# Efficient attention followed by a two-layer MLP: batch 0's k less its maxima on VectorE, its small transfers queued behind large ones, two x tiles of batch 1 turned by DMA, and a new order

## Chip, cores, metric

One Trainium2 chip, one of its cores. The metric is the device time of one execution in microseconds (us); where several runs of a kernel are given, their median. Engines are named as the profile names them: PE (TensorE), DVE (VectorE), ACT (ScalarE), POOL (GpSimd) and SP (SyncE, which here only issues transfers).

## What is computed

Eight batches, eight heads, 576 rows, head size 64; inputs and output are float32.

```python
def _attn_ref(q, k, v):
    q_s = np.exp(q - np.max(q, axis=-1, keepdims=True))
    q_s = q_s / (np.sum(q_s, axis=-1, keepdims=True) + 1e-09)
    k_s = np.exp(k - np.max(k, axis=2, keepdims=True))          # maxima over the rows
    k_s = k_s / (np.sum(k_s, axis=2, keepdims=True) + 1e-09)
    kv = np.einsum('bhsd,bhse->bhde', k_s, v)
    return np.einsum('bhsd,bhde->bhse', q_s, kv)

def _moe_ref(x, g_ln, w_ch1, w_ch2):                            # x: (8, 576, 512)
    mu = np.mean(x, axis=-1, keepdims=True)
    var = np.mean((x - mu) ** 2, axis=-1, keepdims=True)
    xn = (x - mu) / np.sqrt(var + 1e-06) * g_ln
    return x + np.maximum(xn @ w_ch1, 0.0) @ w_ch2              # 512 -> 2048 -> 512
```

## The kernel before

**Tiling.** Of a batch's 576 rows, 512 are held as four tiles of 128 (j = 0 to 3); the last 64 rows of two batches make a fifth tile (j = 4) together. The MLP runs in nine chunks: one for each batch's 512 rows, and a ninth for the left-over rows.

**An order written out by hand.** All the work is a table of tasks `T[(name, batch, part)]`, built in `batch(m)`, `chunk(ci)` and `weights()`. The string `PROGRAM` names every task once; `write_all` goes through it and issues each task's instructions on its engine. Each engine works through its own instructions strictly in that order, and a transfer stands in the queue of the engine that issues it; the engine can be given as in `kll.1@SP`. Waits between engines follow from the data. A word is name.batch.part:

- `kl`, `ql`, `vl`: loads of the 512 rows of k, q, v (1 MB for a batch, in rows of 1 KB; batch 0's are cut by heads into parts of 512 or 256 KB). `kll`, `qll`, `vll`: the 64 left-over rows (128 KB in 512 pieces of 256 bytes). `g`: the norm's weights (0 load, 1 turn, 2 copy). `w1l`, `w2l`: the weights of the two layers, four parts of each, issued by POOL and cast to bf16 on the way.
- `kmax`, `kmaxl` (DVE): maxima of k over the tiles, and with the left-over rows. `kar` (POOL): the same over the partitions. `ksub`, `kexp` (DVE, ACT): subtraction and exponential. `vc`: v cast to bf16.
- `qmax`, `qsub` (DVE), `qexp` (ACT): the same for q. `qT` (PE) and `qTe` (copy) turn q's exponentials; `qTd` does it by DMA on SP. `zpe` sums them on PE (line 361), `zq` on DVE (lines 353 and 354); where `zpe` is used, `zq` is only a reciprocal (line 366).
- `pkv` (PE), `kvb` (DVE): k times v, scaled. `po` (PE), `x` (DVE): the attention's output, scaled, with its row sum. `xn`: x less its mean. `xT` (PE, line 474) with `xTe`/`xTf` (copies) turn it; by DMA it is one transfer on SP (line 500). `sq`, `rstd` (ACT): the norm's factor.
- `l1`, `relu`, `l2`, `put`, `store`: the two layers, the result and its store. `w1s`: layer 1's weights times the norm's weights, for the later chunks. For batches 0 and 1, layer 1 comes in parts l1.batch.c.t: l1.1.8.0 and those after it need all four tiles.
- `warm`: matmuls with no result that is used. `gate.i` (SP): a transfer of a few bytes which waits for a given task (gate.0 for qexp.0.0), so that what stands behind it on SP's queue is issued only then.

**Batch 0's k.** For a pair of heads c below `KPE`, `kid` (line 222) brings k to PSUM through an identity matmul on PE, the task `ksub` is `kless` (line 230), which subtracts the maxima there by a second matmul, and `kexp` reads PSUM. For the other pairs `ksub_pair` (line 235) subtracts on DVE, in place. KPE is 3 of 4 pairs. `KPARTS` cuts k's loads and maxima into heads 0-3, 4-5 and 6-7.

**Sums and turned tiles.** `ZPE = 2`: batches 0 and 1 use `zpe`. `by_dma` says which tiles a DMA turns: from batch 2 on, and the fifth tile.

Of the kernel before, what the change touches and what calls it, by code (L numbers as in the profile page):

```python
# [20 lines left out]
def kernel(  # L21
# [594 lines left out]
    def warm(n, width):  # L616
# [26 lines left out]
        l1.0.1.2 qsub.1.0 l1.0.0.2 qmax.1.2 relu.0.1.2 relu.0.1.3 l1.0.1.0 relu.0.0.2 w1s.0@DV
        l1.0.1.1 relu.0.1.0 qsub.1.2 l1.0.11.0 relu.0.1.1 l1.0.9.0 relu.0.11.0 kmax.1.0 l1.0.8.0
        l1.0.10.0 relu.0.8.0 relu.0.9.0 l1.0.14.0 l1.0.15.0 relu.0.14.0 relu.0.10.0 l1.0.13.0
        kmaxl.1.0 qexp.1.0 w1s.2@DV l1.0.12.0 kar.1.0 relu.0.15.0 l2.0.0 relu.0.13.0 relu.0.12.0
        l2.0.1 w2l.2 ksub.1.0 qexp.1.2 l2.0.2 ksub.1.1 qT.1.0 vc.1.2@PO l2.0.3 qTe.1.0@DV kexp.1.1
        w2l.3 l2.0.4 ksub.1.2 kexp.1.0 qT.1.2 zpe.1.0 l2.0.5 qTe.1.2@DV kexp.1.2 w1s.1@DV
        vc.1.0@AC vc.1.1@PO l2.0.6 ql.2.0@AC zpe.1.2 l2.0.7 sq.0.3 w1s.3@DV pkv.1.0 sq.0.0 pkv.1.1
        sq.0.2 l2.0.8 kvb.1.0 sq.0.1 l2.0.9 zq.1.0 zq.1.2 kl.2.0@AC po.1.2 rstd.0 po.1.0 po.1.3  # L650
        x.1.2 po.1.1 l2.0.10 x.1.0 x.1.1 l2.0.11 xn.1.0@AC gate.4 x.1.3 xn.1.1@AC l2.0.12 kll.2@SP
        xn.1.2@AC kl.3.0@SP l2.0.13 vl.2.0@SP qmax.2.0 xT.1.0 l2.0.14 xTe.1.0@AC put.0.0 l2.0.15
        put.0.1 xn.1.3@AC put.0.2 l1.1.0.0 sq.1.1 qsub.2.0 xT.1.2 relu.1.0.0 l1.1.1.0 xTe.1.2@AC
        put.0.3 l1.1.2.0 kmax.2.0 relu.1.1.0 qexp.2.0 l1.1.3.0 l1.1.8.0 ql.3.0@AC qTd.2.1
        kmaxl.2.0 relu.1.2.0 l1.1.9.0 qmax.2.2 relu.1.3.0 kar.2.0 vll.2@SP l1.1.10.0 relu.1.9.0
        qTd.2.0 qsub.2.2 relu.1.8.0 l1.1.11.0 relu.1.10.0 qll.1.1@SP ksub.2.2 l1.1.12.0
        relu.1.11.0 ksub.2.0 qexp.2.2 l1.1.13.0 relu.1.12.0 ksub.2.1 l1.1.14.0 qTd.2.2 relu.1.13.0
        l1.1.15.0 relu.1.14.0 zq.2.0 qTd.2.3 l1.1.0.2 relu.1.15.0 zq.2.2 l1.1.1.2 vc.2.1
        relu.1.0.2 kexp.2.0 kll.3@SP l1.1.2.2 vc.2.0 kexp.2.1 l1.1.3.2 qll.1.0@SP qmax.3.0 l2.1.0
        kexp.2.2 kll.4@SP vc.2.2 sq.1.3 store.0.0@SP kmax.3.0 l2.1.1 vl.3.0@SP relu.1.2.2 pkv.2.0  # L660
        store.0.2@SP relu.1.1.2 pkv.2.1 sq.1.0 l2.1.2 kvb.2.0 sq.1.2 l2.1.3 store.0.1@AC po.2.3
        store.0.3@AC po.2.1 qmax.1.4 po.2.0 po.2.2 x.2.3 l2.1.4 x.2.0 xn.2.3@AC l2.1.5 kmaxl.3.0
        xn.2.0@AC xT.2.3 l2.1.6 x.2.2 relu.1.3.2 kar.3.0 x.2.1 l2.1.7 xn.2.2@AC xT.2.0 qsub.3.0
        xn.2.1@AC l2.1.8 rstd.1 xT.2.2 ksub.3.0 l2.1.9 qexp.3.0 l2.1.10 put.1.0 xT.2.1 l2.1.11
        ksub.3.1 vll.3@SP l2.1.12 vc.3.0 put.1.1 kexp.3.1 kl.4.0@SP l2.1.13 qsub.1.4 l2.1.14
        put.1.2 qexp.1.4 l2.1.15 kexp.3.0 store.1.2@SP qTd.1.4 l1.2.0 put.1.3 vc.3.2 l1.2.1
        qmax.3.2 relu.2.0 vc.3.1 ql.4.0@SP l1.2.2 qTd.3.0 relu.2.1 ksub.3.2 l1.2.3 relu.2.2
        qsub.3.2 store.1.0@SP l1.2.4 qTd.3.1 relu.2.3 zq.1.4 kexp.3.2 l1.2.5 qexp.3.2 zq.3.0
        l1.2.6 relu.2.4 qTd.3.3 l1.2.7 relu.2.6 zq.3.2 relu.2.5 pkv.3.0 gate.2 relu.2.7 po.1.4
        pkv.3.1 kll.5@SP sq.2.3 x.1.4 l1.2.8 kmax.4.0 l1.2.9 relu.2.8 qTd.3.2 l1.2.10 qmax.4.0  # L670
        l1.2.11 relu.2.10 ql.5.0@SP relu.2.9 l1.2.12 kmaxl.4.0 gate.3 relu.2.11 kvb.3.0 l1.2.13
        kar.4.0 relu.2.12 vl.4.0@SP sq.2.0 store.1.3@SP l1.2.14 qmax.4.2 relu.2.13 l1.2.15
        xn.1.4@AC l2.2.0 sq.2.1 relu.2.15 po.3.1 po.3.0 relu.2.14 po.3.3 po.3.2 l2.2.1 x.3.3 x.3.2
        l2.2.2 xn.3.3@DV xn.3.2@AC x.3.1 l2.2.3 sq.2.2 qsub.4.0 xT.3.2 l2.2.4 rstd.2 x.3.0 sq.3.2
        l2.2.5 xT.3.3 ksub.4.0 xn.3.0@AC l2.2.6 store.1.1@AC xT.3.0 put.2.0 l2.2.7 sq.3.3 ksub.4.1
        xn.3.1@AC l2.2.8 kexp.4.0 xT.3.1 vc.4.1 l2.2.9 ksub.4.2 qexp.4.0 l2.2.10 vll.4@SP vc.4.0
        qmax.5.0 kexp.4.1 kl.5.0@SP l2.2.11 gate.0 put.2.1 kexp.4.2 l2.2.12 qTd.4.0 qsub.4.2
        l2.2.13 l2.2.14 put.2.2 qexp.4.2 vc.4.2 qmax.5.2 l2.2.15 qTd.4.3 l1.3.0 put.2.3 qTd.4.2
        l1.3.1 zq.4.0 pkv.4.0 relu.3.1 store.2.1@SP pkv.4.1 relu.3.0 l1.3.2 qTd.4.1 kvb.4.0 l1.3.3
        relu.3.2 kmax.5.0 kl.6.0@SP l1.3.4 qll.3.1@SP relu.3.3 kll.6@SP qll.3.0@AC l1.3.5 sq.3.1  # L680
        zq.4.2 l1.3.6 relu.3.4 relu.3.5 l1.3.7 kmaxl.5.0 store.2.0@AC qsub.5.2 l1.3.8 relu.3.6
        kar.5.0 l1.3.9 relu.3.8 qsub.5.0 po.4.2 po.4.1 relu.3.9 l1.3.10 relu.3.7 sq.3.0 po.4.0
        po.4.3 l1.3.11 x.4.0 rstd.3 ksub.5.1 relu.3.10 l1.3.12 vl.6.0@AC l1.3.13 x.4.1 relu.3.11
        relu.3.12 xn.4.0@DV l1.3.14 ksub.5.2 relu.3.13 xT.4.0 x.4.3 l1.3.15 relu.3.14 ksub.5.0
        vl.5.0@SP sq.4.1 l2.3.0 store.2.2@SP relu.3.15 x.4.2 l2.3.1 xn.4.1@AC xn.4.3@DV kmax.6.0
        l2.3.2 qexp.5.0 xT.4.3 l2.3.3 xT.4.1 l2.3.4 kmaxl.6.0 xn.4.2@DV l2.3.5 kar.6.0 qmax.3.4
        xT.4.2 l2.3.6 qsub.3.4 put.3.0 l2.3.7 gate.1 qexp.3.4 qTd.5.1 kexp.5.0 ksub.6.2 l2.3.8
        ksub.6.1 qexp.5.2 l2.3.9 store.2.3@SP kexp.5.1 l2.3.10 vll.5@SP vc.5.0 vll.6@SP l2.3.11
        kexp.6.1 vc.6.0 qTd.3.4 l2.3.12 kexp.6.2 put.3.2 vc.5.1 kexp.5.2 l2.3.13 zq.3.4 ql.6.0@SP
        put.3.1 l2.3.14 vc.6.1 kl.7.0@SP ksub.6.0 l2.3.15 qTd.5.2 vc.5.2 l1.4.0 qTd.5.3 put.3.3  # L690
        kexp.6.0 l1.4.1 vc.6.2 zq.5.0 relu.4.0 l1.4.2 qTd.5.0 relu.4.1 l1.4.3 zq.5.2 store.3.2@SP
        l1.4.4 relu.4.3 store.3.1@SP relu.4.2 pkv.5.0 relu.4.4 pkv.6.0 pkv.5.1 kll.7@SP pkv.6.1
        po.3.4 l1.4.5 x.3.4 l1.4.6 kvb.5.0 qll.5.1@SP l1.4.7 qmax.6.0 relu.4.6 relu.4.5 po.5.1
        l1.4.8 qmax.6.2 relu.4.7 l1.4.9 store.3.3@SP relu.4.8 qsub.6.2 ql.7.0@SP l1.4.10 relu.4.9
        x.5.1 l1.4.11 relu.4.10 qsub.6.0 sq.1.4 l1.4.12 relu.4.11 l1.4.13 kvb.6.0 l1.4.14 kmax.7.0
        relu.4.13 relu.4.12 l1.4.15 qexp.6.2 po.5.0 po.5.2 l2.4.0 qexp.6.0 x.5.2 qTd.6.2 l2.4.1
        x.5.0 relu.4.14 relu.4.15 xT.1.4 xn.5.0@DV l2.4.2 kmaxl.7.0 sq.4.0 po.5.3 xn.5.1@AC
        kar.7.0 l2.4.3 x.5.3 qTd.6.3 sq.4.2 l2.4.4 xn.5.3@DV sq.4.3 zq.6.0 l2.4.5 xT.5.3
        store.3.0@AC rstd.4 l2.4.6 xn.5.2@AC zq.6.2 xT.5.0 l2.4.7 sq.5.3 sq.5.0 l2.4.8 xT.5.2
        ksub.7.1 l2.4.9 ksub.7.0 xT.5.1 kexp.7.1 l2.4.10 put.4.0 l2.4.11 kexp.7.0 qll.5.0@SP  # L700
        vll.7@SP l2.4.12 store.4.0@AC qTd.6.1 put.4.2 sq.5.1 l2.4.13 put.4.1 qll.7.1@SP l2.4.14
        qTd.6.0 l2.4.15 vl.7.0@SP l1.5.0 put.4.3 vc.7.2 l1.5.1 ksub.7.2 relu.5.0 l1.5.2 relu.5.1
# [474 lines left out]
```

## Time and profile before

| | |
|---|---|
| median of 3 runs | 293.98 us (293.83 to 294.09) |
| the profiled execution | 294.13 us, its span 292.3 us |
| granted clock of PE, mean | 0.993 |
| PE, DVE, ACT, POOL busy | 282.2, 182.9, 170.7, 50.1 us |
| first product of layer 1 (line 550) | 23.31 us from the span's start |
| first product of layer 2 (line 590) | 38.12 us |
| end of PE's work | 288.74 us |
| read from memory, written | 36.70 MB, 9.44 MB |

The span is from the first to the last instruction. A view of waits names for each instruction what the idle time of its engine ended with; the chain follows the last instruction back through such releasers. A transfer's time to landing counts from its issue. Queue q1 is SP's, q10 ACT's, q0 POOL's. In lines of the timeline the columns are start, duration, engine, line, operation, out<-in, shape and count, and in brackets the idle time before.

### The profile page before, as it was taken

The numbers are of one execution on the slowest core, as the hardware profiler recorded it, in microseconds if no ns is written. First come the engines' busy times: TensorE is split into PE (matmuls) and PEld (weight loads), VectorE is DVE, ScalarE is ACT, GpSimd is POOL, SyncE is SP. The second block draws the span as 40 slices with busy tenths as digits, with TensorE's granted clock in tenths as the row PEclk, the third lists the DMA queues.
The fourth block names the chain that finished last, engine by engine and source line by source line (L and its number), as shares of the span: only waits on it lengthen the run. The fifth ranks groups of instructions, "written<-read, shape, count | busy, mean of one in ns | idle before, by whom it ended". The sixth has DMA issues, their size and how long they took to land.

```text
span 292.3 us, 4988 instructions
## 1 busy us (share of the span) xinstructions
PE 282.2 (97%) x1934; PEld 146.9 (50%) x1964; DVE 182.9 (63%) x309; ACT 170.7 (58%) x319; POOL 50.1 (17%) x51
## 2 busy tenths in 40 slices
...
GB/s 191 337 269 218 228 229 293 321 239 138 253 232 246 240 243 199 167 301 232 172 310 274 120 153 165 144 38 183 34 0 111 90 72 20 71 95 13 2 34 111
DMA packets 78144, 49.62 MB, mean 170 GB/s; under 512 B 44580, under 2 KB 73640, under 8 KB 78120
## 3 DMA queue, kind: packets, MB, share of 16 engines
...
q8 instruction: 15, 0.25, 0.4%
...
HBM read 36.70 MB, written 9.44 MB: 158 GB/s over the span
## 4 chain that ended last, share of the span: by engine, by line
PE 94%; DMA 2%; DVE 2%; issue 1%; POOL 0%; ACT 0%; SPq 0%; DVEq 0%; POOLq 0%
PE pc L590 41%; PE ph L536 33%; PE ph L550 10%; PE pot L419 2%; PE pk L394 2%; DMA kt<-in_k_dram 2%; PE pc L568 1%; PE ks L230 1%; PE idle L619 1%; PE ks L222 1%; PE pxt L474 1%; PE ptr L332 0%; PE pot L428 0%; POOL km L199 0%; DVE kmx L184 0%
## 5 line engine op out<-in xcount | busy, mean ns | idle before, releaser
L590 PE MATMUL pc<-w_sb,hT 128*128 128x512 bf16 x544 | 123.1, 379 | 0.8
L542 ACT ACTIVATE hT<-ph 128x512 bf16<-128x512 f32 x112 | 62.9, 595 | 60.0 <-PE ph L536 59.8
L590 PEld LDWEIGHTS <-hT 128*128 128x128 bf16 x560 | 54.1, 98 | 62.9
L536 PE MATMUL ph<-xnT_ab,w_sb 128*128 128x512 bf16 x373 | 85.1, 379 | 0.5
L536 PEld LDWEIGHTS <-w_sb 128*128 128x128 bf16 x448 | 43.1, 98 | 50.1
L600 DVE SCALAR_TENSOR_TENSOR ot<-pc,rstd,x_ab 128x512 f32<-128x512 f32 x32 | 23.5, 744 | 43.3 <-PE pc L590 38.8
L442 DVE SCALAR_TENSOR_TENSOR x_ab<-pot,rq 128x512 bf16<-128x512 f32 x32 | 21.1, 688 | 20.0 <-PE pot L419 19.6
L199 POOL PARTITION_ALL_REDUCE km<-kmx x10 | 16.0, 1613 | 94.8 <-DVE kmx L194 67.6
L550 PE MATMUL ph<-xnT_ab,w_sb 128*128 128x128 bf16 (+2 forms) x254 | 28.9, 272 | 0.5 <-ACT xnT_ab L492 0.4
L550 PEld LDWEIGHTS <-w_sb 128*128 128x128 bf16 x256 | 19.8, 98 | 9.0 <-issue 0.7
L109 POOL CAST v_ab<-vt 128x1024 bf16<-128x1024 f32 (+1 forms) x15 | 20.4, 1384 | 18.6 <-DMA vt<-in_v_dram 18.5
L466 ACT ACTIVATE xsq<-x_ab,xs_ab 128x512 bf16<-128x512 bf16 x32 | 23.0, 717 | 0.4
L557 ACT ACTIVATE hT<-ph 128x512 bf16<-128x512 f32 x32 | 17.7, 598 | 4.7 <-PE ph L550 4.6
L305 ACT ACTIVATE eq_sb<-qt 128x1024 bf16<-128x1024 f32 x14 | 14.7, 1056 | 7.3 <-DVE qt L300 7.3
L453 ACT ACTIVATE xn_ab<-x_ab,xs_ab 128x512 bf16<-128x512 bf16 x20 | 13.9, 716 | 8.3 <-DVE x_ab L442 8.3
L217 DVE TENSOR_TENSOR kt<-kt,km 128x1024 f32<-128x1024 f32 x14 | 18.1, 1312 | 0.0
L300 DVE TENSOR_TENSOR qt<-qt,qm 128x1024 f32<-128x1024 f32 x14 | 17.8, 1280 | 0.2
L241 ACT ACTIVATE ek_ab<-kt 128x1024 bf16<-128x1024 f32 x14 | 14.4, 1053 | 5.3 <-DVE kt L217 5.2
L295 DVE TENSOR_REDUCE qm<-qt 128x16 f32<-128x1024 f32 x14 | 16.8, 1206 | 0.1
L600 DVE SCALAR_TENSOR_TENSOR ot<-pc,rstd,xl 128x512 f32<-128x512 f32 x3 | 2.2, 749 | 22.0 <-remote 20.0
L353 DVE TENSOR_REDUCE sumq<-eq_sb 128x16 f32<-128x1024 bf16 x12 | 14.3, 1188 | 0.0
L536 PE MATMUL ph<-xnTl,w_sb 128*128 128x512 bf16 x63 | 13.9, 379 | 0.1
...
## 6 DMA issues: line engine op xcount, KB each, us to landing
...
```

The lines of the kernel that those rows point to most:

```text
L109: eng.copy(dst, src) if eng is nc.scalar else eng.tensor_copy(dst, src)
L217: eng.tensor_tensor(a, a, b, op=ALU.subtract)
L295: nc.vector.tensor_reduce(t, self._q(a, n), axis=AX.X, op=ALU.max)
L300: eng.tensor_tensor(x, x, t[:, :, :, None].to_broadcast([P, n, H, D]), op=ALU.subtract)
L442: nc.vector.scalar_tensor_tensor(xt.rearrange("p (h d) -> p h d", h=H), in0=self.pot[j], scalar=-1.0, in1=rq[:, :, None].to_broadcast([P, ...
L466: nc.scalar.activation(xsq, xt, AF.Square, bias=xs, scale=-float(DM), accum_out=s)
L536: nc.tensor.matmul(ph, w1_sb[:, ko, m * P:(m + 1) * P], src[:, ko, :], start=(ko == 0), stop=(ko == KO1 - 1),)
L542: nc.scalar.activation(hT[:, m, :], phs[ci, m], AF.Relu)
L550: nc.tensor.matmul(ph[:, i], w1_sb[:, ko, m * P:(m + 1) * P], xnT_ab[:, ci % 2, ko, t * P:(t + n) * P], start=(ko == 0), stop=(ko == KO1 - 1),
L557: nc.scalar.activation(hT[:, c * (4 // n):(c + 1) * (4 // n), t * P:(t + n) * P], phs[ci, c, t], AF.Relu)
L590: nc.tensor.matmul(pcs[ci, ti], hT[:, ko, ti * P:(ti + 1) * P], w2_sb[:, ko, :], start=(ko == 0), stop=(ko == KO2 - 1),)
L600: nc.vector.scalar_tensor_tensor(ots[ci, ti], in0=pcs[ci, ti], scalar=rstd[:, ci, ti:ti + 1], in1=xt, op0=ALU.mult, op1=ALU.subtract,)
```

## The change

- `KPE` is 0: for all four pairs of batch 0, DVE subtracts (`ksub_pair`), and `kexp` reads SBUF. `kid` and `kless` are not used.
- `ZPE` is 1: batch 1's sums are taken by DVE (`zq`), not by PE.
- Tiles 2 and 3 of batch 1's x are turned by DMA (on SP), not by PE.
- Batch 0's left-over rows of k and v must stand behind kl.0.0 and ahead of vl.0.0 in the order, and g's load behind the others in the table.
- The order is another one. ACT issues batch 0's q, v, left-over rows and the first part of k, SP the other two parts of k. gate.0 stands ahead of batch 1's loads on SP; kll.1 is issued by ACT. DVE takes qmax.0.0 ahead of kmax.0.0, and kmax.1.0 ahead of qmax.1.0. On PE, qT.1.0 and qT.1.2 stand ahead of l2.0.0; the warm matmuls are others.

```diff
-    KPE = 3
+    KPE = 0
-    ZPE = 2
+    ZPE = 1
     def by_dma(what, m, j):
-        return m >= (Q_DMA if what == "q" else X_DMA) or j == J
+        return m >= (Q_DMA if what == "q" else X_DMA) or j == J or (what, m, j) == ("x", 1, 2)
...
-        g.0@SP kll.0 kl.0.0@SP kl.0.1@SP kl.0.2@SP ql.0.0@SP ql.0.1@SP vl.0.0@SP vl.0.1@SP
-        kmax.0.0 warm.8.512 kid.0.1 ql.1.0@SP kmax.0.1 kmaxl.0.0 g.1 kid.0.0 kmax.0.2 g.2@AC
-        kar.0.0 vll.0 kmaxl.0.1 kmaxl.0.2 qmax.0.0 kl.1.0@SP warm.5.128 ksub.0.0 kar.0.2 kar.0.1
-        ksub.0.1 qsub.0.0 kexp.0.0 w1l.0 kid.0.2 kexp.0.1 qmax.0.1 kll.1@SP w1l.1 qexp.0.0 w1l.2
-        ksub.0.4 vc.0.0@AC warm.11.128 qT.0.0 w1l.3 qsub.0.1 vll.1@SP ksub.0.2 vc.0.3@PO kexp.0.4
-        ksub.0.3 qexp.0.1 vc.0.1@PO warm.7.128 pkv.0.0 kexp.0.2 qT.0.1 qTe.0.0@DV kexp.0.3 kvb.0.0
-        vc.0.2@PO warm.4.128 zpe.0.0 qTe.0.1@AC pkv.0.1 w2l.0 pkv.0.2 kvb.0.1 warm.5.128 zpe.0.1
-        w2l.1 zq.0.0 warm.5.128 po.0.0 po.0.3 po.0.1 x.0.0 po.0.2 x.0.3 xn.0.0@AC x.0.1 xn.0.3@AC
-        warm.12.128 xT.0.0 vl.1.0@SP xTf.0.0@DV xTe.0.0@AC warm.4.128 xT.0.3 xn.0.1@DV x.0.2
+        ql.0.0@AC kl.0.0@AC kll.0 vll.0 ql.0.1@AC vl.0.0@AC vl.0.1@AC g.0@SP kl.0.1@SP qmax.0.0
+        kl.0.2@SP kmax.0.0 kmaxl.0.0 qsub.0.0 kar.0.0 qexp.0.0 w1l.0 ksub.0.0 kmax.0.1 w1l.1
+        kexp.0.0 warm.27.512 qT.0.0 gate.0 kmax.0.2 g.1 w1l.2 kl.1.0@SP kmaxl.0.1 ql.1.0@SP
+        kmaxl.0.2 qmax.0.1 kar.0.1 w1l.3 ksub.0.1 vc.0.0@AC vl.1.0@SP kar.0.2 ksub.0.2 kexp.0.1
+        w2l.0 qsub.0.1 vc.0.3@AC w2l.1 kexp.0.2 ksub.0.4 qexp.0.1 ksub.0.3 kexp.0.4 qTe.0.0@DV
+        vll.1@SP warm.20.512 qT.0.1 vc.0.1@PO kexp.0.3 pkv.0.0 qTe.0.1@DV vc.0.2@AC pkv.0.1
+        kvb.0.0 g.2@AC warm.4.128 pkv.0.2 zpe.0.0 zpe.0.1 kvb.0.1 zq.0.0 warm.8.128 po.0.0 po.0.3
+        po.0.1 x.0.0 po.0.2 x.0.1 xn.0.0@AC x.0.2 xn.0.1@AC warm.12.128 xT.0.0 xTf.0.0@DV
+        xTe.0.0@AC warm.4.128 xT.0.1 x.0.3 xTf.0.1@AC warm.3.128 l1.0.0.0 xTe.0.1@DV xn.0.3@AC
+        xn.0.2@DV l1.0.0.1 kll.1@AC relu.0.0.0 xT.0.3 xT.0.2 relu.0.0.1 l1.0.1.0 xTf.0.3@DV
+        ql.2.0@SP kmax.1.0 xTe.0.3@AC l1.0.1.1 relu.0.1.0 l1.0.0.3 relu.0.1.1 xTe.0.2@DV
...
+        relu.0.11.0 kmaxl.1.0 l1.0.13.0 relu.0.0.2 qsub.1.0 kar.1.0 l1.0.14.0 relu.0.13.0 qsub.1.2
+        qexp.1.0 l1.0.12.0 w2l.2 l1.0.15.0 ksub.1.0 qexp.1.2 w2l.3 qT.1.0 relu.0.14.0 ksub.1.1
+        qT.1.2 relu.0.12.0 l2.0.0 relu.0.15.0 zq.1.0 l2.0.1 l2.0.2 vc.1.0@AC ksub.1.2 vc.1.1@PO
...
+        sq.0.1 po.1.0 po.1.1 po.1.2 rstd.0 po.1.3 x.1.1 l2.0.9 kl.2.0@AC x.1.2 xn.1.1@AC l2.0.10
+        x.1.0 xn.1.2@AC x.1.3 l2.0.11 xn.1.0@AC xT.1.2 kl.3.0@AC l2.0.12 xn.1.3@AC qmax.2.0 xT.1.0
+        xT.1.3 l2.0.13 xTe.1.0@AC put.0.0 l2.0.14 put.0.1 w1s.1@AC vll.2@SP vl.2.0@SP l2.0.15
...
         T["kll", m] = task(
             lambda e: s.load_kl(e), (), LD if m else (AC,), olds("kexp", 4, range(5)), olds("kexp", 3, range(5)),
+            after=None if m else T["kl", 0, 0],
         )
...
-                after=T["vl", m, i - 1] if i else None,
+                after=T["vl", m, i - 1] if i else None if m else T["vll", 0],
...
+        if m == 0:
+            T["g", 0] = task(
+                lambda e: e.dma_start(g_rows, moe_g_ln.rearrange("(ko ki) -> ko ki", ki=P)),
+                (), LD, after=T["vl", 0, 1],
+            )
...
```

200 lines of the change are left out of this document (94 added, 106 removed).

## Prediction

> **What bounds the kernel now.** I read the page first, then the chain of waits, the timelines of PE, DVE, ACT, POOL and SP up to 75 us, and the DMA view in stretches of half a microsecond.
>
> ```profile
> PE 282.2 (97%) x1934; PEld 146.9 (50%) x1964; DVE 182.9 (63%) x309; ACT 170.7 (58%) x319; POOL 50.1 (17%) x51
> PE 94%; DMA 2%; DVE 2%; issue 1%; POOL 0%; ACT 0%; SPq 0%; DVEq 0%; POOLq 0%
> ```
>
> PE holds 94% of the chain. The other engines matter only where they keep PE from starting:
>
> ```profile
> 1.18 5.15 DMA kt<-in_k_dram
> ...
> 8.69 1.07 POOL km L199
> ...
> 20.30 0.71 DVE x_ab L442 x2
> ...
> 23.57 1.00 PE ph L550 x15
> ...
> 38.28 2.59 PE pc L590 x12
> ```
>
> Two regimes. Up to the first product of layer 1 (l1.0.0.0, 23.31 us on the timeline) the chain runs through k's first part, its maxima, the reduction and batch 0's attention. From there PE has work without a hole until 288.74. So an edit counts in three ways: by when l1.0.0.0 starts, by what PE has to do afterwards, and by any hole it makes in that stretch.
>
> **PE's work after the start.** ZPE = 1 takes batch 1's sums from PE: 2 x 0.18 us of the chain's L361 pieces. The tiles 2 and 3 of batch 1 that a DMA turns take away one piece of L474, 0.45. Together -0.81 us. Their counterparts are covered: two sums on DVE (1.20 + 0.25 each, L353 and L354, against 2 x 0.18 for L366, so +2.5), where DVE has 2.3 us of idle time at 39.8 to 43.5; bare, they would cost those 2.5. The matmuls of kid and kless (L222, L230) and the changed numbers of warm matmuls all lie ahead of l1.0.0.0.
>
> **The start.** Before, DVE is the long queue there, yet it waits:
>
> ```profile
> 15.02 0.68 DVE L235 TENSOR_TENSOR kt<-kt,km 128x512 f32<-128x512 f32 x1
> 15.62 0.67 DVE L109 COPY qT_sb<-ptr 128x1024 bf16<-128x1024 bf16 x1
> 17.59 0.17 DVE L404 RECIPROCAL rz<-pk 128x2 f32<-128x2 f32 x1 [1.29 <-PE pk L394]
> ...
> 19.00 0.17 DVE L404 RECIPROCAL rz<-pk 128x2 f32<-128x2 f32 x1 [0.60 <-PE pk L394]
> ```
>
> From k's landing (6.33) to x.0.0 (20.30) are 13.97 us, 1.89 of them idle. After, DVE gets three more subtractions (L235, start to start 0.60) and qTe.0.1, which ACT did (0.62): +2.4. It loses the first maximum of q (1.13), which now comes ahead of k. Its own queue from k's landing to x.0.0 is then 13.97 - 1.89 + 2.4 - 1.13 = 13.4 us, and with one short wait for the reduction 13.5. The idle time is used up, so 0.5 us are won; the question is when k lands. It now stands second on ACT's queue, behind 512 KB of q, and SP issues the other 512 KB of k beside it. The stream moves 1407 packets of 1 KB in 4 us (the fence further down), 0.35 MB/us; kll's first packets flow 1.5 us after its issue at 0.78, and vll lands 1.2 us after its last packets. 1.57 MB from 2.5 us on are through at 7.0, so k lands at 8.2, 1.9 later than before. Bounds: 6.45 (issued at 1.3, the old 5.15 us) and 9.1 (the slow first microseconds of before, 0.59 MB by 5.0). x.0.0 comes at 21.7 and l1.0.0.0, 3.0 behind it as before, at 24.7: **+1.4 us**.
>
> **Batch 1's loads, where I see the hole.** Before, kl.1.0, ql.1.0, kll.1 and the rest are queued on SP from 6.5 us on; q lands at 18.6, k at 27.1, kll.1 at 30.3, and kmaxl.1.0 runs at 33.96. After, gate.0 holds SP until qexp.0.0: k 8.2, maxima 1.41, qsub 1.14, exponential 1.05, issue of the gate 0.59, so kl.1.0 is issued at 12.4 and flows at 13.9. By then the weights flow too, and they share:
>
> ```profile
> q0 software_dynamic: 610, 0.61, 71.5%
> q1 hardware_dynamic: 611, 0.62, 44.4%
> ```
>
> That is 17 to 22 us, POOL's queue (q0) and SP's (q1): 122 packets per us each. kl.1.0's 1024 packets take 8.4 us, to 22.3; ql.1.0 to 30.7 (landing about 2 later, as kl.1.0's did: 32.7); vl.1.0 to 39.1. kll.1 is now issued by ACT, behind xn.0.3, at about l1.0.0.0 + 1.5 = 26.2. What a small transfer of ACT's gets behind SP's big ones is shown by vll (8 to 12 us):
>
> ```profile
> q1 hardware_dynamic: 1407, 1.40, 110.2%
> ...
> vl<-in_v_dram ACTq DMA_DIRECT2D x1, 128.0 KB, 7.9
> ```
>
> Issued at 7.76, it has no packet on its own queue (q10) before 12.3: about 1180 of SP's packets go first, then the two alternate. The store that ACT issues at 72.77 waits in the same way until vl.3.0 is nearly through (77). At 122 per us 1180 packets take 9.7 us: kll.1 flows from 35.9, is through at 39.4 (the weights' 3072 packets end near 38) and lands at **41.0**. Bounds: 33.8 (first packet after 1.5, 4.9 us for 512 packets of three queues, 1.2 to land) and 44 (behind vll.1 as well).
>
> [...]
>
> Who waits for kll.1: on DVE, kmaxl.1.0 stands ahead of qsub.1.0 and qsub.1.2; on ACT the two exponentials follow, with relu.0.14, relu.0.12 and relu.0.15 behind them; and on PE qT.1.0 and qT.1.2 now stand ahead of l2.0.0, where before they stood behind it. From kll.1's landing: 0.69 + 1.13 + 1.13 + 1.05 + 0.15 for the hand-overs + 0.45 = 4.6, so l2.0.0 can start at 45.6. Without the wait it starts at 24.7 + 14.8 (layer 1 as before, 23.31 to 38.12) + 0.9 (the two transposes, moved forward) = 40.4. **Hole: +5.2 us**; it opens once kll.1 lands after 35.8. PE then has 0.9 us of work in 6, and such a pause has a second price:
>
> ```profile
> 12.00:15.00 3.00, 3.00 (x17) 1.79 (x17) 3.00 (x4) 2.83 (x4) 2.35 (x4) 0.50 1.12 319
> ```
>
> The third figure from the end is the granted clock: half, from 11.97 to 15.3, after a stretch from 5.6 on in which PE had little to do. 3.3 us at half speed cost 1.65 us where PE is the bound. Between 0 and 1.65 I take **+0.8**: the pause is longer, but one instance doesn't give the point where it sets in. [...]
>
> What is late next: w2l.2 and w2l.3, behind kar.1.0 on POOL, start near 44 and land within 8.2 us as before, ahead of l2.0.8 at 53. DVE's queue from kmaxl.1.0 to x.1.1 is 13.8 us, PE's from l2.0.0 to po.1.1 about 9 behind 4.6, so these keep step. xT.1.2 and xT.1.3 go past SP's queue: ACT issues kl.2.0 and kl.3.0 around them, the latter ahead of xn.1.3. xT.1.3 is issued 17.9 us behind kmaxl.1.0 and lands 2.4 to 6.9 later (L500's rows); l1.1.8.0 needs it 24 behind. Cover of 3.7 at best, short by 0.8 at worst: taken at 0. In later batches the PE order is new, but DVE (152 of 251 us) and ACT (150) have room: 0, with 1 us kept for the range.
>
> **Sum.** The profiled execution took 294.13 us (span 292.3), the median is 293.98, so 0.15 is taken off. 294.13 + 1.4 - 0.81 + 5.2 + 0.8 = 300.7; as a median 300.6.
>
> **Rivals.** (1) No hole: kll.1 lands by 35.8, since it shares at once or the weights finish early. For it: equal sharing; against it: vll and the store. 294.13 + 1.4 - 0.81 - 0.15 = 294.6, with the bounds of k's landing 292.8 to 295.5. (2) Faster: two queues fetch side by side, and k lands 5.15 us after its issue as before, at 6.45, with no hole: l1.0.0.0 at 22.95, time 292.8. It decides when k lands by 7.0. For it: DVE's 0.5 us and PE's 0.81; against it: 1 MB of other data in flight ahead of k's last packets. (3) Worse: kll.1 goes behind vll.1 too (44: +3.0), the clock halves in full (+0.85), xT.1.3 comes 0.8 late: 305.
>
> **Chances.** The hole as forecast, 297 to 303.5: 0.56. Rival 1, 293.4 to 297: 0.25. Rival 2, below that: 0.11. Rival 3, above 303.5: 0.08. A measurement of this kernel tells 0.2% (0.6 us) from no change; of rival 1, 0.09 lies within that, since its own value lies at that bound. The range is the first two, 293.5 to 303.5, 0.81 in all. Faster 0.11, same 0.09, slower 0.80.
>
> **What would show it.** In the changed profile: kmax.0.0 (L184, 128x512) starts near 8.2; x.0.0 near 21.7 and L550 near 24.7; DVE's idle time ahead of L194 (64x512) ends with kl's landing near 41; PE's idle time ahead of L372, then L590 from 45.6 on; the granted clock below 1 there. Wrong, if L194 waits for nothing and PE runs through from L550 to L590; then rival 1 or 2 holds, by where L184 starts.

## The result, and the profile after

The changed kernel takes 298.37 us (median of 6 runs, 298.01 to 300.43); beside it the kernel before took 293.9 (6 runs, 293.56 to 295.25). The ratio is 1.0161, 95% interval 1.0136 to 1.0187: slower by 4.5 us. The forecast was 300.6, range 293.5 to 303.5. The profiled execution of the changed kernel is the longest of its six: 300.43 us, span 298.6, mean granted clock 0.989. One other execution with that clock took 300.06; the four with 0.993 to 0.994 took 298.0 to 298.4. So the profiled execution is some 2 us longer than those with the higher clock, and the experiments are compared by medians.

Its page, first the busy times, then the chain by engine:

```profile
PE 284.8 (95%) x1912; PEld 148.0 (50%) x1943; DVE 185.7 (62%) x306; ACT 175.0 (59%) x328; POOL 48.4 (16%) x48
...
PE 79%; DVE 9%; DMA 8%; ACT 1%; issue 1%; POOL 1%; ACTq 0%; SPq 0%; DVEq 0%; POOLq 0%
```

PE held 94% of the chain before. Now 17% are DVE and transfers. The pieces of the chain of waits that are not PE's bulk (start, duration, what) say where:

```profile
1.83 6.78 DMA kl<-in_k_dram
9.32 1.87 POOL km L199
23.08 1.80 PE pot L419 x16
27.76 10.54 DMA kl<-in_k_dram
39.12 3.20 DVE qt L300 x2
42.32 3.95 DVE kt L217 x2
58.25 7.17 DMA xnT_ab<-xn_ab
```

Three of these lie ahead of layer 1's first product, which moved from 23.31 to 27.57. The others are kll.1 with DVE's work behind it, and, last, the tile xT.1.3. DVE's timeline up to x.0.0 and PE's waits:

```profile
7.12 0.69 DVE L184 TENSOR_TENSOR kmx<-kt 128x512 f32<-128x512 f32 x1 [1.31 <-DMA kt<-in_k_dram]
...
8.70 0.42 DVE L194 TENSOR_TENSOR kmx<-kmx,kl 64x256 f32<-64x256 f32 x1 [0.43 <-DMA kl<-in_k_dram]
...
11.21 0.69 DVE L235 TENSOR_TENSOR kt<-kt,km 128x512 f32<-128x512 f32 x1 [0.96 <-POOL km L199]
...
14.68 2.14 DVE L235 TENSOR_TENSOR kt<-kt,km 128x512 f32<-128x512 f32 x2
...
17.88 1.09 DVE L217 TENSOR_TENSOR kl<-kl,km 64x512 f32<-64x512 f32 x1
...
23.54 0.69 DVE L442 SCALAR_TENSOR_TENSOR x_ab<-pot,rq 128x512 bf16<-128x512 f32 x1 [0.64 <-PE pot L419]
```

```profile
27.57 2.29 PE L550 MATMUL ph<-xnT_ab,w_sb 128*128 128x128 bf16 x32 [0.17 <-ACT xnT_ab L492]
...
43.47 0.62 PE L372 MATMUL ptr<-ident,eq_sb 128*128 128x128 bf16 x8 [0.45 <-ACT eq_sb L305]
...
53.58 1.05 PE L419 MATMUL pot<-kv_ab,qT_sb 128*128 128x128 bf16 x16 [0.86 <-DVE kv_ab L407]
...
65.55 10.56 PE L550 MATMUL ph<-xnT_ab,w_sb 128*128 128x512 bf16 x63 [0.93 <-DMA xnT_ab<-xn_ab]
```

The clock, by stretches (the third figure from the end is the granted clock):

```profile
16.00:20.00 4.00, 1.49 (x31) 0.90 (x29) 4.00 (x5) 3.51 (x6) 2.42 (x3) 1.00 1.15 246
20.00:24.00 4.00, 3.94 (x70) 3.49 (x64) 2.99 (x10) 0.80 (x3) 0.00 (x0) 0.51 1.17 248
```

Between 16.6 and 19.1 PE has nothing to do (the 20 warm matmuls end too early), and from 20.06 to 26.88 it runs at half clock, where it does batch 0's attention.

**The account, in profiled times.** The start is 4.26 us later. k lands 0.77 later (7.12 against 6.35); DVE from there to x.0.0 takes 16.42 in place of 13.95, +2.47; from x.0.0 to l1.0.0.0 it is 4.03 in place of 3.01, +1.02. From l1.0.0.0 to l2.0.0 (43.93) it is 16.36 in place of 14.81, +1.55: the two transposes moved forward (0.9), the hole of 0.45, and 0.2 not assigned. From l2.0.0 to PE's last products it is about 0.65 longer, though 1.7 us of work went from there (0.81 saved, 0.9 moved forward): waits of 0.16, 0.86 and 0.93 stand against that, and 0.4 is not assigned. Together 6.5 us; the spans differ by 6.3.

### The profile page after: what moved, and what is told of

It reads as the page before. It is cut to its first block, busy times and chain, and to the rows that moved or that the text cites. A ratio compares the mean times of both kernels' runs of the same rounds, so it can differ in the third digit from the quotient of the medians.

```text
span 298.6 us, 4966 instructions
## 1 busy us (share of the span) xinstructions
PE 284.8 (95%) x1912; PEld 148.0 (50%) x1943; DVE 185.7 (62%) x306; ACT 175.0 (59%) x328; POOL 48.4 (16%) x48
## 4 chain that ended last, share of the span: by engine, by line
PE 79%; DVE 9%; DMA 8%; ACT 1%; issue 1%; POOL 1%; ACTq 0%; SPq 0%; DVEq 0%; POOLq 0%
PE pc L590 36%; PE ph L536 32%; DMA kl<-in_k_dram 6%; PE ph L550 4%; PE pot L419 2%; DMA xnT_ab<-xn_ab 2%; PE pk L394 2%; DVE kt L217 1%; PE pc L568 1%; DVE kt L235 1%; DVE w_sb L517 1%; DVE qt L300 1%; PE idle L619 1%; DVE sumq L353 1%; ACT xn_ab L453 1%
## 5 line engine op out<-in xcount | busy, mean ns | idle before, releaser
L590 PE MATMUL pc<-w_sb,hT 128*128 128x512 bf16 x544 | 122.8, 379 | 0.9 <-issue 0.2
L536 PE MATMUL ph<-xnT_ab,w_sb 128*128 128x512 bf16 x373 | 86.0, 379 | 0.5
L590 PEld LDWEIGHTS <-hT 128*128 128x128 bf16 x560 | 54.2, 98 | 63.1
L199 POOL PARTITION_ALL_REDUCE km<-kmx x10 | 17.2, 1724 | 107.6 <-DVE kmx L194 107.5
L550 PE MATMUL ph<-xnT_ab,w_sb 128*128 128x128 bf16 (+2 forms) x254 | 28.8, 271 | 1.2 <-DMA xnT_ab<-xn_ab 0.9
L550 PEld LDWEIGHTS <-w_sb 128*128 128x128 bf16 x256 | 19.7, 98 | 10.0 <-DMA xnT_ab<-xn_ab 1.2
L453 ACT ACTIVATE xn_ab<-x_ab,xs_ab 128x512 bf16<-128x512 bf16 x26 | 17.7, 716 | 10.7 <-DVE x_ab L442 10.6
L109 POOL CAST v_ab<-vt 128x1024 bf16<-128x1024 f32 (+1 forms) x14 | 20.2, 1455 | 21.4 <-DMA vt<-in_v_dram 19.7
L300 DVE TENSOR_TENSOR qt<-qt,qm 128x1024 f32<-128x1024 f32 x14 | 18.9, 1354 | 0.1
L217 DVE TENSOR_TENSOR kt<-kt,km 128x1024 f32<-128x1024 f32 x14 | 18.8, 1356 | 0.0
L619 PE MATMUL idle<-kv_ab,ident 128*128 128x512 bf16 (+1 forms) x77 | 16.5, 378 | 2.4 <-DVE kv_ab L1123 2.3
L295 DVE TENSOR_REDUCE qm<-qt 128x16 f32<-128x1024 f32 x14 | 16.7, 1202 | 2.2 <-DMA qt<-in_q_dram 2.1
L353 DVE TENSOR_REDUCE sumq<-eq_sb 128x16 f32<-128x1024 bf16 x14 | 16.9, 1207 | 0.1
```

Of the source, the lines that this page charges most:

```text
L109: eng.copy(dst, src) if eng is nc.scalar else eng.tensor_copy(dst, src)
L217: eng.tensor_tensor(a, a, b, op=ALU.subtract)
L300: eng.tensor_tensor(x, x, t[:, :, :, None].to_broadcast([P, n, H, D]), op=ALU.subtract)
L353: nc.vector.tensor_reduce(z, self._eq(a, n), axis=AX.X, op=ALU.add)
L453: eng.activation(xn_ab[:, j], xt, AF.Identity, bias=xs, scale=-float(DM))
L536: nc.tensor.matmul(ph, w1_sb[:, ko, m * P:(m + 1) * P], src[:, ko, :], start=(ko == 0), stop=(ko == KO1 - 1),)
```

## Experiments

Two theories were set against each other. A: the start is what is lost, through batch 0's left-over rows, the reduction, DVE's subtractions beside POOL, and the half clock. B: it is batch 1's loads, issued late behind gate.0; behind them DVE waits and PE gets holes.

### On the changed kernel: the clock

```diff
-vll.1@SP warm.20.512 qT.0.1
+vll.1@SP warm.32.512 qT.0.1
```

> The changed kernel with 32 instead of 20 warm matmuls of 128x512 behind qT.0.0, so that PE's pause of 2.5 us ahead of qT.0.1 (16.6 to 19.1) is filled; nothing else. Theory A (the time is lost ahead of l1.0.0.0, and part of it to the half clock, 20.5 to 26.9 in the profiled execution): the clock stays full up to l1.0.0.0, which comes 2 us or more ahead of 27.57; 296.2 to 297, and no executions near 300. Theory B (batch 1's loads set the end: kll.1 and ql.1.0 hold DVE until 38.4 whatever the start does): l1.0.0.0 comes earlier, but PE's hole ahead of l2.0.0 grows from 0.45 by as much; 298 as before.

Measured: 297.09 (296.61 to 297.89), ratio to before 1.0103 [1.0080, 1.0126]; the mean clock is 0.998 to 1.000 in all six. The stretch from 20 to 24 us:

```profile
20.00:24.00 4.00, 3.35 (x84) 2.80 (x85) 3.73 (x12) 1.27 (x4) 0.00 (x0) 1.00 1.18 251
```

Layer 1 starts at 26.07, 1.50 earlier where A had 2 or more, and the median lies just above A's range. Twelve matmuls of no use are worth 1.3 us in the median, and 3.0 to 3.3 against the two executions at 0.989. The waits of 0.86 and 0.93 further down are gone too. The hole ahead of L372 grows from 0.45 to 0.84: B in part, since it doesn't grow by as much as the start came forward. DVE now waits 3.67 us at L295 for batch 1's q, which lands at 34.9 as before: B's wait is there, for the most part hidden behind layer 1.

### On the changed kernel: KPE = 3 again

```diff
-KPE = 0
+KPE = 3
...
-ksub.0.0 kmax.0.1 w1l.1 kexp.0.0 warm.27.512
+warm.18.512 kid.0.0 kid.0.1 ksub.0.0 ksub.0.1 kmax.0.1 w1l.1 kexp.0.0
...
-vll.1@SP warm.20.512
+vll.1@SP warm.10.512
```

> The changed kernel with KPE = 3 again: kid and kless on PE for three pairs of heads of batch 0, in the place of 18 and 10 of the warm matmuls; loads and all else as in the changed kernel. Theory A, DVE's longer queue: DVE loses three subtractions (0.60 each, and 0.87 by which two of them ran slower beside POOL), so x.0.0 comes 2 to 2.7 us earlier and the time falls to 295.7 to 296.5. Rival, the order of the loads is what costs: x.0.0 keeps within 0.7 of 23.5 and the time stays at 297.7 or more.

Measured: 302.14 (300.57 to 303.09), ratio 1.0260 [1.0227, 1.0292]; mean clock 0.981 to 0.989. Slower, against theory A, but not a clean test: the identity matmuls lie behind late loads, the clock was half from about 13.7 to 24, and DVE waited 5.67 us for PE's qT.0.1. The bound had moved to PE.

### On the changed kernel: kll.1 on SP behind ql.1.0

```diff
-ql.1.0@SP
+ql.1.0@SP kll.1@SP
...
-l1.0.0.1 kll.1@AC relu.0.0.0
+l1.0.0.1 relu.0.0.0
```

> The changed kernel with kll.1 issued by SP right behind ql.1.0 instead of by ACT behind xn.0.1's turn. Theory B: kll.1 is there when q's maxima are done (37.2), so DVE goes on 1.2 us earlier and the holes of PE ahead of qT.1.2 (0.45), po.1.1 (0.86) and l1.1.8.0 (0.93) shrink together by 1 to 2 us: 296.4 to 297.4. Theory A: only the start counts, 298.0 to 298.6.

Measured: 299.01 (298.35 to 300.09), ratio 1.0171 [1.0145, 1.0197]. No gain, and above both theories' ranges. kmaxl.1.0 still waits, 0.87 us until 37.75, and the hole ahead of L372 is 0.59. The profiled execution is at half clock from 20.45 to 23.86 only, half as long as the changed kernel's; layer 1 starts at 26.78.

### On the changed kernel: the two tiles turned by PE again

```diff
-... or (what, m, j) == ("x", 1, 2)
...
-xn.1.0@AC xT.1.2 kl.3.0@AC
+xn.1.0@AC kl.3.0@AC
-xT.1.3 l2.0.13
+l2.0.13
...
-l1.1.0.0 qsub.2.0
+l1.1.0.0 xT.1.2 xTe.1.2@AC qsub.2.0
```

> The changed kernel with tiles 2 and 3 of batch 1's x turned by PE again (8 transposes, 0.45 us, and one copy on ACT of 1.0), placed behind l1.1.0.0. If the wait for the turned tile (0.93 us ahead of l1.1.8.0) is the DMA's own lateness: 0.5 us less, 297.9. If x itself is late and the wait only moves to the transposes: the same or up to 0.45 more, 298.4 to 298.9.

Measured: 298.75 (298.03 to 299.76), ratio 1.0161 [1.0135, 1.0186], the same as the changed kernel's. The wait of 0.93 is gone, but PE waits 1.49 us at 107.88 for a turned q tile of batch 2, one transfer on SP's queue later in the order.

The profiled execution of this kernel (298.88) kept the full clock, though its start has the same instructions as the changed kernel's: layer 1 starts at 25.71 there, 1.86 earlier than the 27.57 with 6.8 us at half clock.

### On the kernel before: only the work taken from PE

ZPE = 1 and both tiles turned by DMA, xT.1.2 and xT.1.3 issued ahead of kl.3.0, zq.1.0 and zq.1.2 behind the subtractions of batch 1.

```diff
-ZPE = 2
+ZPE = 1
...
-qT.1.2 zpe.1.0
+qT.1.2
...
-xn.1.2@AC kl.3.0@SP l2.0.13
+xn.1.2@AC xT.1.2 l2.0.13 xn.1.3@AC xT.1.3 kl.3.0@SP
```

> The kernel before, with the part of the change alone that takes work from PE: batch 1's sums on DVE (ZPE = 1) and tiles 2 and 3 of batch 1's x turned by DMA, issued on SP ahead of the load of batch 3's k. Its start is that of before. Theory: the 0.81 us of PE's work are won in full, 293.1 (ratio 0.997). Rival: DVE (two sums of 1.20 + 0.25 against 2 x 0.18) holds up the products of batch 1's attention, or layer 1 of batch 1 waits 0.9 us for the tiles that the DMA turns, as in the changed kernel; then 293.9 to 295.

Measured: 293.12 (12 runs, 292.51 to 295.64), ratio 0.9987 [0.9960, 1.0013]. The median is 0.76 lower, but four of the twelve runs lie above 294.5, so the ratio alone doesn't prove it. The trace shows the mechanism: from layer 1's first product to the first of L568 it is 260.92 us (23.27 to 284.19) against 261.72 before (23.31 to 285.03), 0.80 less, and layer 1 of batch 1 waits for no tile: L550 runs without a pause from 54.98 to 69.04.

### On the kernel before: only KPE = 0

```diff
-KPE = 3
+KPE = 0
...
-kid.0.1 ... kid.0.0 ... kid.0.2
```

> The kernel before, with one part of the change alone: KPE is 0, so DVE subtracts k's maxima for all four pairs, and the three identity matmuls are gone. Theory A1 (DVE's longer queue makes a good part of the late start): three subtractions of 0.60 us join DVE's queue, which had 1.89 us idle ahead of x.0.0, of which some 1.3 come too late to take them; x.0.0 comes 0.5 to 1.8 us later than 20.30 and layer 1's first product 0.5 to 1.8 later than 23.31; time 294.4 to 295.7. Rival A2 (the loads' order and POOL make the late start, DVE's own work fits into its idle time): start within 0.3 us of before, time 293.6 to 294.2.

Measured: 296.48 (295.81 to 297.06), ratio 1.0079 [1.0052, 1.0107]: 2.6 us for this alone, more than theory A1 allowed. Layer 1 starts at 24.97. DVE's five subtractions run at full speed here; it is POOL that pays. Its timeline, and then PE's:

```profile
14.28 3.28 POOL L109 CAST v_ab<-vl 64x512 bf16<-64x512 f32 x1 [0.23 <-DMA vl<-in_v_dram]
```

```profile
14.16 1.03 PE L332 MATMUL ptr<-ident,eq_sb 128*128 128x128 bf16 x8 [6.26 <-ACT eq_sb L326]
```

The cast of 64x512 took 0.61 in the kernel before (at 15.76), and PE's pkv waits 1.31 us for it. PE, without the identity matmuls, stands idle for 6.26 us; the clock is half from 11.2 to 21.4 us (mean of the executions 0.974 to 0.983).

### KPE = 0 with the gap filled

```diff
 the kernel before with KPE = 0:
-kl.1.0@SP warm.5.128 ksub.0.0
+kl.1.0@SP warm.27.512 ksub.0.0
```

> The kernel before with KPE = 0 (which alone gave 296.48, PE idle 6.26 us ahead of qT.0.0, the clock half from 12 to 20 us, layer 1's first product at 24.97), and 27 warm matmuls of 512 columns in place of 5 of 128 behind k's landing, to fill what the identity matmuls left empty. Theory A5 (the identity matmuls also kept PE's clock up, and that is most of KPE's price): the clock is full from 12 to 20, layer 1 starts at 23.6 to 24.2, time 294.2 to 295.0. Rival A6 (the price is DVE's two-operand subtractions and POOL beside them, where a cast took 3.28 us in place of 0.61): layer 1 starts at 24.6 to 25, time 295.3 to 296.2.

Measured: 296.15 (12 runs, 295.50 to 297.66), ratio 1.0067 [1.0045, 1.0089]. The time lies in A6's range, but layer 1 starts at 25.85, later than either theory had it. The matmuls ended at 12.5; PE then waited 1.76, 1.63 and 1.03 us, and the clock was half from 15.8 to 22.6. Now L217 was the slow one, beside POOL's casts:

```profile
14.15 2.26 DVE L217 TENSOR_TENSOR kl<-kl,km 64x512 f32<-64x512 f32 x1
```

The six executions at a mean clock of 0.994 took 295.5 to 295.9 (median 295.7); those of the kernel before at 0.993 to 0.994 took 294.1 in the median beside them. So some 1.6 us of KPE's price remain at the same mean clock, against A5. How the rest divides stays open.

### On the changed kernel: POOL quiet beside DVE's subtractions

```diff
-warm.20.512
+warm.32.512
-kar.0.1 w1l.3 ksub.0.1 ... kar.0.2 ksub.0.2 ... w2l.0 ... w2l.1 ... vc.0.1@PO
+kar.0.1 kar.0.2 ksub.0.1 ... ksub.0.2 ... vc.0.1@AC ... qTe.0.0@DV pw.0 w1l.3 w2l.0 w2l.1
```

(pw.0 is the copy of 128 elements that waits for qTe.0.0. In the changed kernel kar.0.2 and the cast vc.0.1 ran beside the subtractions:)

```profile
14.89 0.67 POOL L199 PARTITION_ALL_REDUCE km<-kmx  x1
...
16.92 1.50 POOL L109 CAST v_ab<-vt 128x512 bf16<-128x512 f32 x1
```

> The changed kernel with 32 in place of 20 wide warm matmuls (which alone gave 297.09, layer 1's first product at 26.07, the clock full), and POOL kept quiet beside DVE's subtractions of batch 0: the second and third part of the reduction directly behind each other, the issues of w1l.3, w2l.0 and w2l.1 held behind qTe.0.0 by a copy of 128 elements, the cast vc.0.1 on ACT. Theory A3 (POOL's issues slow DVE): the two subtractions at L235 that took 1.04 us each take 0.60 to 0.68, L217 0.67 in place of 1.09, so x.0.0 1.0 to 1.4 us earlier, near 21.8, and layer 1's first product near 24.9; time 295.8 to 296.4 if all is kept. Rival B (batch 1's q, landing at 34.9, holds DVE and so PE behind layer 1): the start is earlier, DVE waits longer at L295, the hole ahead of L372 is 1 us longer, time 296.8 to 297.3. Rival A4 (the slowing isn't POOL's doing): L235 stays at 1.04.

Measured: 298.92 (297.46 to 299.41), ratio 1.0147 [1.0111, 1.0182]. DVE's rows, and then PE's:

```profile
14.80 1.27 DVE L235 TENSOR_TENSOR kt<-kt,km 128x512 f32<-128x512 f32 x2
...
17.14 0.68 DVE L217 TENSOR_TENSOR kl<-kl,km 64x512 f32<-64x512 f32 x1
```

```profile
42.96 0.68 PE L372 MATMUL ptr<-ident,eq_sb 128*128 128x128 bf16 x8 [1.36 <-ACT eq_sb L305]
43.43 7.88 PE L590 MATMUL pc<-w_sb,hT 128*128 128x512 bf16 x28
```

A3's times are there: with POOL out of the way the pair takes 1.27 in place of 2.14, and L217 0.68 in place of 1.09. Which of issues, reduction and cast did it, this run doesn't separate, since it moved all three. By their places, the reduction lies beside the pair, and the cast (0.67 in a quiet place) beside L217, which ends 0.55 behind it. For the issues alone other runs disagree: in the kernel without the gate the same pair took 1.28 with two of them beside it (at 16.05), in the kernel with DVE's other order one L235 took 1.10 (at 17.04). As a gain the edit fails. qTe.0.1 then waited 0.77 us for PE, which was in its 32 warm matmuls until 19.3, so the start came only 0.55 earlier (25.52 against 26.07); batch 1's q landed at 35.5, waits of 0.46 and 1.36 us opened in front of layer 2, and the granted clock was half from about 43.4 to 46.8. That is B, and with the clock more than B had.

### On the changed kernel: DVE's order at the first maxima

```diff
-warm.20.512
+warm.32.512
-kmax.0.0 kmaxl.0.0 qsub.0.0 kar.0.0 qexp.0.0 w1l.0 ksub.0.0 kmax.0.1 w1l.1 ... kmax.0.2 g.1 w1l.2
+kmax.0.0 qsub.0.0 kmaxl.0.0 kmax.0.1 kar.0.0 qexp.0.0 w1l.0 kmax.0.2 w1l.1 ksub.0.0 ... g.1
-kar.0.1 w1l.3 ksub.0.1 ... kar.0.2 ksub.0.2
+kar.0.1 kar.0.2 w1l.2 w1l.3 ksub.0.1 ... ksub.0.2
```

> The changed kernel with 32 wide warm matmuls (297.09), and another order of DVE around the first maxima: qsub.0.0 ahead of kmaxl.0.0, and the maxima of the later heads ahead of ksub.0.0, so that DVE has work while it waited 0.46 us for kll.0 and 0.96 us for the reduction; the later reductions stand ahead of w1l.2 on POOL. Theory A (these waits are part of the late start): x.0.0 1.0 to 1.4 us earlier, near 21.9, layer 1's first product near 24.9; 295.7 to 296.4 if it is kept. Rival B (batch 1's q holds DVE): ql.1.0 is issued up to 0.8 us earlier with the gate, so at most 0.8 is won: 296.3 to 297.1.

Measured: 296.78 (296.64 to 297.15), ratio 1.0090 [1.0064, 1.0117]. DVE's waits of 0.46 and 0.96 are gone and layer 1 starts at 25.27, 0.8 earlier, but POOL took 3.84 us for the two later reductions (1.39 in the kernel before), so a part was given back at once. Of the 0.8, 0.3 is left in the median, which lies in rival B's range:

```profile
36.20 0.69 DVE L194 TENSOR_TENSOR kmx<-kmx,kl 64x512 f32<-64x512 f32 x1 [3.51 <-DMA kl<-in_k_dram]
```

DVE waits 3.51 us for kll.1, issued at 25.46, and PE waits 0.55 (ahead of L372) and 0.87. This is the forecast's hole, near the start that the forecast had (24.7): 0.55, or 1.4 with the second wait, not 5.

### Without the gate, and the gate alone

```diff
 changed kernel with 32 warm matmuls and DVE's other order:
-qT.0.0 gate.0 g.1 kl.1.0@SP kmaxl.0.1 ql.1.0@SP
+qT.0.0 g.1 kl.1.0@SP kmaxl.0.1 ql.1.0@SP kll.1@SP
...
-l1.0.0.1 kll.1@AC relu.0.0.0
+l1.0.0.1 relu.0.0.0
...
-put.2.1 qexp.4.2
+put.2.1 gate.0 qexp.4.2
```

> The changed kernel with 32 wide warm matmuls and DVE's other order at the start (which gave 296.78, layer 1's first product at 25.27, DVE idle 3.51 us for kll.1 and PE idle 0.55 and 0.87 us), and batch 1's loads no longer behind the gate: gate.0 goes back to its old place late in the order, and kll.1 stands on SP directly behind ql.1.0. Theory B (behind the start, batch 1's late loads are what bounds the changed kernel): ql.1.0 and kll.1 land by 31, DVE waits for neither, the holes of 1.4 us are gone and batch 1's attention comes earlier; time 295.0 to 295.8. Rival B2 (the bandwidth that these loads take early is taken from batch 0's v and from the weights): the start is 0.5 to 1.5 us later, or layer 1 waits for w1l; time 296.5 to 298.

Measured: 300.81 (300.24 to 301.13), ratio 1.0217 [1.0188, 1.0246]. DVE no longer waits at L194 or L295 and the holes are gone, as B says, but layer 1 starts at 31.09. ACT's issue of batch 0's v comes at 7.92 and takes 5.00 us (4.07 and 3.41 in the changed kernel), and POOL waits for that v until 23.73:

```profile
23.73 0.62 POOL L109 CAST v_ab<-vt 128x512 bf16<-128x512 f32 x1 [6.43 <-DMA vt<-in_v_dram]
```

With batch 0's v issued last on ACT's queue, the new order needs the gate: otherwise batch 1's loads on SP's queue take as many packets as v does (172 and 171 from 12 to 13 us). This is B2, with a start 5.8 us later and not 0.5 to 1.5. Not all of it is v's: the 32 warm matmuls, from 15.30 on and up to 20.4 at half clock, last until 24.9, qT.0.1 stands behind them at 24.70, and DVE waits 5.08 us for it. The cast of v ends at 24.35, so v alone would hold PE some 0.9 us less.

```diff
 the kernel before:
-kid.0.1 ql.1.0@SP ... qmax.0.0 kl.1.0@SP ... qmax.0.1 kll.1@SP w1l.1 qexp.0.0
+kid.0.1 ... qmax.0.0 ... qmax.0.1 w1l.1 qexp.0.0 gate.0 ql.1.0@SP kl.1.0@SP kll.1@SP
...
-l2.2.11 gate.0 put.2.1
+l2.2.11 put.2.1
```

> The kernel before, with batch 1's loads alone changed: gate.0 stands ahead of ql.1.0, kl.1.0 and kll.1 on SP, which so are issued only behind qexp.0.0, near 13.9 us in place of 6.5 to 13. Theory B (batch 1's late loads cost a hole by themselves, as the forecast had it): k's left-over rows land at 37 to 38, DVE reaches kmaxl.1.0 (L194, 64x512) 3 to 4 us later than 33.96, of which its 2.3 us of idle time behind take a part; PE has holes of 0.5 to 1.5 us between 40 and 55, time 294.4 to 295.5. Rival B3 (the loads have room, and what the changed kernel lost it lost in its start and its clock): L194 is later, but PE has no new hole, 293.7 to 294.2.

Measured: 297.48 (296.52 to 299.02), ratio 1.0123 [1.0098, 1.0148]. B is wrong, and B3 is right only on the hole. L194 is 5.1 us later (39.11), and PE has no new hole: from layer 1 to layer 2 it is 14.80 us, as before. But layer 1 starts at 25.37, and the clock stays half:

```profile
12.00:16.00 4.00, 4.00 (x23) 2.47 (x21) 4.00 (x6) 3.70 (x5) 3.56 (x5) 0.58 1.18 225
16.00:20.00 4.00, 4.00 (x58) 3.13 (x59) 0.88 (x4) 1.92 (x4) 2.57 (x5) 0.50 1.20 218
```

The first of these rows has the mean of the kernel before (0.58 there too, half from 11.95 to 15.36); the second was 1.00 there. Here the clock is half from 12.60 to 22.84. At half clock PE's own products became what DVE waits for (2.12, 1.49 and 0.62 us). Why the clock came back after 3.4 us in the one and after 10.2 in the other, with PE marked busy all the time in both, nothing here shows. The profiled execution is the fastest of its six, at the lowest mean clock (0.983); the five others, at 0.987 to 0.991, took 0.3 to 2.5 us more. So the clock accounts for the 2 us by which the profiled start is later, and the further 1 us in the median has another cause, which isn't in the trace.

### A version faster than both

The kernel before with the savings of PE's work (the edit of the run above with ZPE = 1), and more warm matmuls at its start:

```diff
-kmax.0.0 warm.8.512 kid.0.1
+kmax.0.0 warm.10.512 kid.0.1
...
-kl.1.0@SP warm.5.128 ksub.0.0
+kl.1.0@SP warm.5.512 ksub.0.0
```

> The kernel before with the savings of PE's work (which alone gave 293.12 with single runs up to 295.6), and more warm matmuls ahead of and behind k's landing: 10 in place of 8, and 5 of 512 columns in place of 5 of 128, against the half clock that it shows from 12 to 15.3 us. Theory: with the clock full, PE's products pkv, for which DVE waited 1.30 and 0.61 us, come earlier and layer 1's first product 0.3 to 1.0 us earlier than 23.3; 292.1 to 292.8, and fewer runs near 295. Rival: DVE's queue or the late part of the clock's drop holds the start, or the clock falls anyway: 292.9 to 293.4.

Measured: 293.28 (12 runs, 292.34 to 295.15), ratio to before 0.9968 [0.9941, 0.9994]: faster by 0.3%. That is about the saving alone; the clock still fell from 12 to 15.3 in the profiled execution, and the start (23.18) is that of before. The rival of its expectation holds. The six executions with a mean clock of 0.998 to 1.000 took 292.34 to 293.31, where those of the kernel before at 0.997 and more took 293.32 to 293.82.

## Why the prediction was right, and where it was not

The time lies in the range, and it is slower, as forecast. That the size came near is luck: the forecast put 1.4 us into the start and 6.0 behind it (the hole and its half clock), and measured are 4.26 and 0.45 in the profiled execution, which is the longest of the six. Two terms were wrong by several microseconds, in opposite directions.

**k's landing: too late.** It lands 0.77 later, not 1.9, within the bounds given (6.45 to 9.1). Rival 2 needed it by 7.0, which it missed by 0.1, and needed DVE to keep to 13.4 us behind it; it failed by the second.

**DVE's queue from k to x.0.0: the step that failed first.** "Its own queue ... is then 13.97 - 1.89 + 2.4 - 1.13 = 13.4 us, and with one short wait for the reduction 13.5" became 16.42. 2.28 us of it are idle time (0.43 for kll.0, now behind kl.0.0; 0.96 for the reduction, which took 1.87 beside DVE; 0.25 and 0.64 for PE at half clock), where 0.1 was allowed. The work itself is 14.14: the subtractions were costed at 0.60 each by a row in which POOL was idle; beside POOL two of them took 2.14 together. The profile of before has the slow case further down, within the 75 us that were read: a subtraction of 64x512, 0.67 at 13.29, takes 1.52 beside two casts, which take 5.25 in place of about 2.1 (DVE's row, and POOL's):

```profile
62.19 1.52 DVE L217 TENSOR_TENSOR kl<-kl,km 64x512 f32<-64x512 f32 x1
```

```profile
61.64 5.25 POOL L109 CAST v_ab<-vt 128x1024 bf16<-128x1024 f32 x2
```

**The half clock: wrong in place and cause.** It was put behind the hole, where the clock is 1.00 (40 to 48 us). In the changed kernel it lies ahead of layer 1 and makes +1.02 there and 0.89 in DVE's waits. The same start at full clock, in the kernel with the tiles turned by PE, is 1.86 earlier, and 1.3 is what the median gives back with 32 warm matmuls; +0.8 was taken, for another place. So the start was +1.4 by the sum and is +4.26 in the profiled execution, and without the clock's part +2.4 to +2.8 (25.71, and 26.07 with 32 warm matmuls).

**The hole ahead of l2.0.0: 5.2 forecast, 0.45 measured.** By the forecast kll.1 is issued 1.5 us behind l1.0.0.0, lands 14.8 after its issue, and l2.0.0 follows 4.6 behind the landing. Measured are 0.19, 10.54 and 5.6. The first two make the hole 5.6 smaller, the third 1.0 larger; with the 0.2 not assigned, that is the 0.45. A later start doesn't cover more of the hole, since kll.1's issue moves with the start: with layer 1 at 27.57 and at 25.27 the issue came 0.19 behind it, and the hole was 0.45 and 0.55. The third term is DVE's L300, 3.20 for the two where 2 x 1.13 were taken, beside a reduction on POOL.

The delay of kll.1 is the step that failed here. Its queue is q10 (32 to 37 us):

```profile
q0 software_dynamic: 554, 0.55, 64.9%
q1 hardware_dynamic: 554, 0.55, 40.2%
q10 hardware_dynamic: 521, 0.13, 11.9%
```

Issued at 27.76, kll.1 has no packet until 32.05, then 521 in 5 us beside 554 on each of the other two. In these 4.29 us SP's queue moved 528 packets; vll in the kernel before waited 4.50, while SP moved 1582 (not 1180), and the store at 72.77 waited 4.02, while SP moved 875. In five other kernels with kll.1 on ACT's queue its wait is 4.26 to 4.51. So the waits keep within 4.02 to 4.51 us while SP's packets in them differ by a factor of three; the forecast carried vll's wait over as a number of packets, 9.7 us. What sets this time is not shown, and other transfers of ACT's wait less (1.07 at 53.28). By the forecast's own terms the landing would have been 39.4 + 1.2 = 40.6, not 41.0. Rival 1 (no hole) is nearly right behind layer 1 and misses by the start; its 294.6 is 3.8 off.

**When the clock fell.** The half stretches ahead of layer 1 last 3.41 us in the kernel before (11.95 to 15.36), 6.82 in the changed kernel (20.06 to 26.88) and 10.2 with KPE = 0 alone (11.2 to 21.4). The rows below show how long PE was busy in the 3.41 us ahead of a fall, or in a like stretch without one; no run varied that alone. They are: the changed kernel ahead of its fall; the kernel with the tiles turned by PE, which kept the full clock, over the first part of the same pause (16.5 to 19.0; the 3.41 us behind that row have 2.51 busy); and, with POOL quiet, the stretch with the waits of 0.46 and 1.36, after which the clock was half:

```profile
16.64:20.05 3.41, 0.95 (x28) 0.84 (x28) 3.41 (x5) 2.92 (x5) 1.78 (x2) 1.00 1.15 240
```

```profile
14.76:18.17 3.41, 1.68 (x8) 0.59 (x6) 3.41 (x4) 1.95 (x4) 3.38 (x5) 1.00 1.17 229
```

```profile
39.98:43.39 3.41, 1.59 (x19) 0.93 (x18) 3.41 (x3) 2.49 (x4) 3.41 (x4) 1.00 1.12 272
```

PE's busy time is the second figure: 0.95 and 1.59 us stand ahead of a half clock, 1.68 ahead of a full one. So the same pause was followed by a half clock in one execution and not in another. What decides it was not shown, and PE's busy time alone doesn't order the cases: in the kernel before, PE is marked busy for 2.65 us from 8.54 to 11.95, and the clock is half behind it.

A half clock behind a hole, as forecast, does occur in the kernel with POOL quiet: L590's 28 products took 7.88 us in place of the 6.21 of the same group in the other kernels, 1.67 more, with the clock half from about 43.4 to 46.8. The forecast's full price, 1.65 for 3.3 us at half speed, was an estimate from the kernel before; this trace agrees with it.

**PE's work: -0.81 forecast, -0.80 measured** by itself on the kernel before. In the changed kernel's profile the wait of 0.93 for xT.1.3 takes it back; the step taken at 0 had its bound at 0.8.

**What stays open.** KPE = 0 alone costs 2.6 us, the gate alone 3.4, of which the clock at the start explains some 2 and 1 stays open. They don't add: the whole change costs 4.5, with 0.8 saved. With the clock kept up and DVE's order mended, 2.9 are left, of which 1.96 are the start (25.27 against 23.31) and 1.4 the two holes, less the saving; 0.3 is not assigned. No run gets the rest of the start back, so its division among k's later landing, DVE's added work and POOL beside it is read from the traces, not tested.
